# A fused convolution and two-layer MLP on one core: the third chunk's convolution taps added up on VectorE and transposed in blocks

## The chip, the cores and the metric

One core of a Trainium2 chip runs the whole kernel: TensorE (matmuls), VectorE, ScalarE and GpSimd, with SyncE issuing most transfers. The metric is device time in microseconds of one execution; the profile's span is a little shorter than that time. Smaller is better.

## What is computed

```python
def _attn_ref(x, weight_gen):            # x (2, 4096, 192), weight_gen (2, 4096, 8, 7)
    w = exp(weight_gen - max(weight_gen)); w = w / (sum(w) + 1e-09)
    x_unf = x_pad[:, idx, :].reshape(B, S, K, H, group)
    out = np.einsum('bshk,bskhg->bshg', w, x_unf)
def _moe_ref(x, w_gate, w_val, w_out):   # 192 -> 1536 -> 192
    gate = 1.0 / (1.0 + np.exp(-(x @ w_gate)))
    return gate * (x @ w_val) @ w_out
def _moe2_ref(x, w_in, w_out):           # 192 -> 2048 -> 192
    h = x @ w_in
    return h * np.cos(h) @ w_out
```

A convolution with 7 taps whose weights are a softmax per token and head is followed by a gated layer (layer 1) and a layer with h cos h (layer 2), all on 8192 tokens of 192 numbers.

## The kernel before

**Chunks and steps.** The tokens lie 64 to a partition and are worked off in 16 chunks of 512 (`NCH`, `TC` = 4 tokens per partition). A chunk needs its convolved input transposed, features on partitions: the tile `xT`. Layer 1 of a chunk is 12 steps, layer 2 is 8; `segments` (lines 646 to 651) orders them as layer 1 of chunks 0 and 1, then layer 2 of chunk 0, layer 1 of chunk 2, layer 2 of chunk 1, and so on: layer 1 runs two chunks ahead (`LEAD = 2`). All orders are as the code issues them (`manual_schedule`); every engine works its own list in order.

**A step.** Each step is a hidden group of 18 matmuls into two PSUM banks (`hidden`, line 442), then work on the four other engines, then, some steps later, one out group of 10 matmuls in layer 1 and two in layer 2 (`out_matmuls`, line 461). Operands are split in a high part (`gh`, made by ScalarE, line 619) and a low part (`gl`, made by GpSimd, line 620, 128x512 from two SBUF operands) and both are multiplied. Of the ten matmuls the first four read gh, the next two gl. There are four banks for hidden groups (`ps_h`), so a group can start when the group two steps before has been read for the last time; in layer 2 this is VectorE's product at line 609.

**In a layer-2 step** (lines 849 to 870) VectorE rounds (592, 595, 600), ScalarE takes the sine (605), VectorE multiplies twice (609); the first tile's gh and gl follow at once, the second tile's one step later (`pending`). `finish1` ends a chunk's layer 1: two sums on VectorE (471) in the step in which its last out group runs, then a copy on ScalarE (482) with a sum on GpSimd (483), then two splits (123) and three transfers, `exchange` (368), one stage per step (`later`).

**The input of layer 1.** Chunks 0, 1 and 2 keep the seven products of the convolution apart (`conv_products`, line 311: four in a tile `big`, two in `pr`, one in `acc`), and TensorE adds them up by transposing all seven into the same banks: 7 x 16 matmuls by the identity (`transposes`, line 334). ScalarE and VectorE empty these banks (357, 363), and two transfers complete `xT`. For chunk 2 this stands at the last step of chunk 1's layer 1. Chunks 3 to 14 (`by_blocks`, line 490) go another way: VectorE adds the products as they come (308), transposes 32x32 blocks (395), ScalarE and GpSimd split the result in `hb` and `lb` (402, 404), and SyncE places it with 16 transfers of 48 KB and four more between the halves of `xT` (410, 417, 418). `blocks_ops` does that in five stages, one per layer-2 step.

**Shared buffers.** `big` of chunk 2 lies where `xT` of chunk 1's layer 2 comes to lie (tag `xA`, one buffer); `tr` and `hb` take the places of the two `pr`, `lb` that of `acc`.

Of the kernel before, what the change touches and what calls it, by code (L numbers as in the profile page):

```python
# [14 lines left out]
ALU = mybir.AluOpType  # L15
# [14 lines left out]
def dyn_conv_glu_cos_mlp(  # L30
# [11 lines left out]
    nc = tc.nc  # L42
    B, S, D = x.shape
    H, K = weight_gen.shape[2], weight_gen.shape[3]
# [5 lines left out]
    NCH = T // TC  # L50
# [225 lines left out]
    att = {}  # L276
# [12 lines left out]
    def product_tile():  # L289
        return apool.tile([P, TC, D], F32, name="pr", tag="pr", bufs=2)  # L290
# [20 lines left out]
    def conv_products(c):  # L311
# [3 lines left out]
        for k, pr in enumerate(att[c]):  # L315
            tap(c, k, pr)
            yield

    def banks(name):

        return [ps_h.tile([P, N], F32, name=name, tag="h") for _ in range(2)]
# [68 lines left out]

    def blocks_ops(c):

        src = att[c][0]
        tr = product_tile()
        nc.vector.transpose(
            out=tr.rearrange("p t d -> p (t d)").rearrange("p (b t r) -> p b t r", t=TC, r=BL),
            in_=src.rearrange("p t (b r) -> p b t r", r=BL),
        )
        yield
        hi = apool.tile([P, TC, D], F32R, name="hb", tag="pr", bufs=2)  # L400
        lo = apool.tile([P, TC, D], F32R, name="lb", tag="acc", bufs=1)
        nc.scalar.activation(out=hi, in_=tr, func=AF.Copy)
        yield
        nc.gpsimd.tensor_tensor(out=lo, in0=tr, in1=hi.bitcast(F32), op=ALU.subtract)
        xt = xT[1, c] = tpool.tile([P, 2, NQ, N], F32R, name="xT", tag="xB")
        for x, piece in (0, hi), (1, lo):
            v = piece.bitcast(F32).rearrange("p t d -> p (t d)").rearrange("p (q e n) -> p q e n", q=NQ, e=2)
            for e in range(2):
                for b in range(P // BL):
                    nc.sync.dma_start(  # L410
                        out=xt[e * BL:(e + 1) * BL, x, :, b * P:(b + 1) * P].bitcast(F32),
                        in_=v[b * BL:(b + 1) * BL, :, e],
                    )
            yield
        low, top = HALVES
        for x in range(2):
            nc.sync.dma_start(out=xt[top, x, 0:2].bitcast(F32), in_=xt[low, x, 1:3].bitcast(F32))
            nc.sync.dma_start(out=xt[top, x, 2].bitcast(F32), in_=xt[low, x, 0].bitcast(F32))
# [70 lines left out]

    def by_blocks(c):  # L490

        return LEAD < c < NCH - 1

    def finish2(c):
        va, vc = sums(1.0)
# [150 lines left out]
    LEAD = 2  # L646
# [20 lines left out]
    def do_side(k, budget):  # L667
        i = 0
        while i < len(side):
            lo, hi, cst, fn = side[i]  # L670
            if lo > k:
                i += 1
            elif hi > k and cst > budget:
                break
            else:
                side.pop(i)
                fn()
                budget -= cst
# [19 lines left out]
    def run(ops):  # L698
        for f in ops:
            f()  # L700
        ops.clear()

    with tc.manual_schedule():
# [86 lines left out]
        inputs = {seg_start[1, c - 1] + J1 - (1 if c > 1 else AHEAD): c for c in range(1, NCH)}  # L790
# [9 lines left out]
        blocks = None  # L800
# [6 lines left out]
        for k, st in enumerate(steps):  # L807
            layer, c, j = st.layer, st.c, st.j
            ended = None
            if layer == 1:  # L810
                run(pending)
                do_side(k, 2.5 if k < J1 else 2.0 if k < seg_start[2, 1] else 0.5)
                st.mm_hidden()
                old = bool(waiting) and (waiting[0].layer, waiting[0].c) != (layer, c)
                if old or len(waiting) >= 2 and OUTS[j]:
                    ended = out_products()
                st.gate()
                run(late)
                if j == FINAL and final:
                    next(final)  # L820
                if j == st.nj - 1:
                    nc.scalar.activation(out=warm, in_=sin_bias, func=AF.Sin)
                pending.append(st.product1)
                pending.append(lambda st=st: st.halves(0))
                if ended:
                    ended.finish()
                if k in inputs and by_blocks(inputs[k]):
                    blocks = blocks_ops(inputs[k])
                    next(blocks)
                    next(blocks)  # L830
                    pending.pop(0)()
                    out_products()
                    pending.pop(0)()
                    out_products()
                elif k in inputs:
                    c1 = inputs[k]
                    ops = transpose_ops(att[c1], c1)
                    pending.pop(0)()
                    next(ops)
                    if c1 == 1:  # L840
                        next(decoding)
                        run(late)
                    next(ops)
                    out_products()
                    pending.pop(0)()
                    for _ in ops:
                        pass
                    out_products()
            else:
                st.mm_hidden()  # L850
                if blocks and next(blocks, blocks) is blocks:
                    blocks = None
                n = sum(q.layer == 1 for q in waiting)
                for _ in range(-(-n // (2 - j)) if n else len(waiting) >= 2):
                    ended = out_products() or ended
                if final:
                    for at in (0, 0, 3) if c < NCH - 1 else (2, 3, 4, 5):
                        if j == at and next(final, final) is final:
                            final = None
                st.reduce(ended and ended.finish)  # L860
                run(pending)
                st.cosine()
                for i, r in st.tiles_of():
                    st.product2(i, r)
                    if i == 0 or st is steps[-1]:
                        st.halves(i, r)
                    else:
                        pending.append(lambda st=st: st.halves(1))
                do_side(k, 0.5)
                run(late)  # L870
            if todo:
                todo.pop(0).load(nc.sync)
            waiting.append(st)
            if later and not ended and (k < J1 or k >= s2 or j in (3, 5, 7, 9)):
                if next(later[0], later) is later:
                    later.pop(0)
            if layer == 1 and j == st.nj - 2 and c + 2 < NCH:
                load_x(c + 2)
                if c + 4 in group_at and group_at[c + 4] > 2:
                    load_group(group_at[c + 4], "wf")  # L880
            if layer == 2 and c == 0 and j == 5:
                load_group(2, "wf")
# [35 lines left out]
```

## Time and profile before

| | |
|---|---|
| median of 3 runs | 1217.94 us (1216.75 to 1218.92) |
| profiled execution | 1217.96 us, span 1216.2 us |
| granted TensorE clock | 0.992 of full speed |
| TensorE, VectorE busy | 98%, 75% |
| ScalarE, GpSimd busy | 66%, 64% |
| mean DMA rate | 59 GB/s |

The table on the page gives shares over the whole span. Which engine sets the end in a given stretch is read from the timeline and from the waits: an engine that never waits there sets it. In the rows, PE is TensorE's matmuls, PEld its weight loads, DVE VectorE, ACT ScalarE, POOL GpSimd and SPq SyncE's queue.

### The profile page before, as it was taken

How to read it: one execution, taken by the hardware profiler on the slowest of the kernel's cores; microseconds unless marked ns; L12 is line 12 of the kernel's file. 1: busy time of each engine (PE TensorE's matmuls, PEld its weight loads, DVE VectorE, ACT ScalarE, POOL GpSimd, SP SyncE). 2: the span in 40 equal slices, each digit the busy share in tenths (PEclk: the TensorE clock that was granted, in tenths of full speed). 3: DMA queues.
4: the chain of work that ended last, by engine and by line, in shares of the span. 5: the costliest groups of instructions: out<-in, count | busy, mean ns of one | idle time of the engine just before them, and what ended most of it. 6: DMA issues, size and time to landing. Idle time of an engine off the chain costs nothing.

```text
span 1216.2 us, 26799 instructions
## 1 busy us (share of the span) xinstructions
PE 1191.1 (98%) x10624; PEld 1000.3 (82%) x10624; DVE 911.2 (75%) x1274; ACT 797.6 (66%) x1317; POOL 775.3 (64%) x573
## 2 busy tenths in 40 slices
PE   6899999999999999999999999999999999999997
PEld 5688988888888888888888888888888888899885
DVE  7957888777887777887777887776877777682676
ACT  6776847658475665857557585765847667485675
POOL 3968757657576565756656676565757657574563
PEclk8999999999999999999999999999999999999999
DMA  9912104123030311303123140311313132020011
GB/s 252 247 51 77 39 1 106 32 58 68 34 79 15 99 37 47 79 33 64 30 77 60 35 86 13 85 35 56 74 34 65 28 81 44 7 53 1 14 29 26
DMA packets 97246, 71.41 MB, mean 59 GB/s; under 512 B 57444, under 2 KB 80994, under 8 KB 97120
## 3 DMA queue, kind: packets, MB, share of 16 engines
q1 hardware_dynamic: 96208, 68.57, 24.0%
q8 instruction: 83, 1.36, 0.5%
q10 hardware_dynamic: 912, 1.13, 0.4%
q14 instruction: 43, 0.35, 0.1%
HBM read 30.33 MB, written 6.29 MB: 30 GB/s over the span
## 4 chain that ended last, share of the span: by engine, by line
PE 84%; DVE 1%; ACT 1%; issue 0%; POOL 0%; DVEq 0%; ACTq 0%
PE ph L442 47%; PE po L461 37%; DVE wk L581 0%; DVE acc L308 0%; ACT gh L619 0%; DVE pr L282 0%; POOL gl L620 0%; ACT wk L605 0%; DVE wk L592 0%; DVE wk L609 0%; DVE wk L595 0%; PE pf L532 0%; DVE wk L600 0%; DVE gl L620 0%; ACT wk L578 0%
## 5 line engine op out<-in xcount | busy, mean ns | idle before, releaser
L620 POOL TENSOR_TENSOR gl<-wk,gh 128x512 fp32r<-128x512 f32 x446 | 617.8, 1392 | 402.5 <-ACT gh L619 345.6
L442 PE MATMUL ph<-xT,unit 64*128 64x512 f32 x5760 | 764.0, 388 | 5.1 <-DVE wk L581 3.6
L442 PEld LDWEIGHTS ph<-xT,unit 64*128 64x128 f32 x5760 | 599.6, 185 | 112.0 <-DVE wk L581 7.0
L461 PE MATMUL po<-gh,outu 64*128 64x512 f32 x2688 | 547.8, 387 | 2.0 <-ACT gh L619 1.9
L461 PE MATMUL po<-gl,outu 64*128 64x512 f32 x1792 | 467.9, 388 | 3.1 <-POOL gl L620 3.0
L461 PEld LDWEIGHTS po<-gh,outu 64*128 64x128 f32 x2688 | 405.9, 184 | 49.9 <-ACT gh L619 2.7
L619 ACT ACTIVATE gh<-wk 128x512 fp32r<-128x512 f32 (+1 forms) x450 | 283.1, 629 | 222.6 <-DVE wk L581 188.2
L461 PEld LDWEIGHTS po<-gl,outu 64*128 64x128 f32 x1792 | 319.9, 184 | 37.4 <-POOL gl L620 6.2
L581 DVE TENSOR_TENSOR wk<-ph,wk 128x512 f32<-128x512 f32 x192 | 131.8, 687 | 135.3 <-ACT wk L578 128.5
L609 DVE SCALAR_TENSOR_TENSOR wk<-ph,wk 128x512 f32<-128x512 f32 (+1 forms) x258 | 168.5, 687 | 33.7 <-ACT wk L605 33.7
L605 ACT ACTIVATE wk<-wk,sin_bias 128x512 f32<-128x512 f32 (+1 forms) x258 | 172.9, 713 | 28.0 <-DVE wk L595 20.4
L578 ACT ACTIVATE wk<-ph 128x512 f32<-128x512 f32 x192 | 113.5, 591 | 60.6 <-PE ph L442 59.7
L592 DVE TENSOR_SCALAR wk<-ph 128x512 f32<-128x512 f32 x129 | 88.0, 682 | 70.7 <-PE ph L442 70.7
L599 ACT ACTIVATE wk<-ph 128x512 int32<-128x512 f32 x129 | 75.9, 588 | 63.4 <-PE ph L442 62.6
L282 DVE TENSOR_TENSOR pr<-xp,sm 128x768 f32<-128x768 f32 x84 | 105.9, 1262 | 0.0
L308 DVE TENSOR_TENSOR acc<-acc,pr 128x768 f32<-128x768 f32 x78 | 103.7, 1330 | 0.4
L595 DVE SCALAR_TENSOR_TENSOR wk<-wk,ph 128x512 f32<-128x512 f32 x129 | 88.1, 683 | 4.4
L600 DVE TENSOR_TENSOR wk<-wk,ph 128x512 f32<-128x512 int32 x129 | 87.3, 677 | 0.3 <-ACT wk L599 0.3
L471 DVE SCALAR_TENSOR_TENSOR va<-po,va 128x512 f32<-128x512 f32 x32 | 22.0, 688 | 37.5 <-PE po L461 34.3
L505 POOL TENSOR_TENSOR vc<-vc,vs 64x256 f32<-64x256 f32 x30 | 31.3, 1044 | 1.9 <-ACT vs L504 0.8
L470 ACT ACTIVATE va<-po 128x512 f32<-128x512 f32 x32 | 19.1, 597 | 19.3 <-PE po L461 19.0
L123 POOL TENSOR_TENSOR unit<-wf,unit 128x768 fp32r<-128x768 f32 (+1 forms) x11 | 22.2, 2023 | 13.6 <-ACT unit L121 13.6
(68 smaller groups left out, 499.6 us busy)
## 6 DMA issues: line engine op xcount, KB each, us to landing
xT<-xT SPq DMA_DIRECT2D x78, 256.0 KB, 3.8
xp<-in_x_dram SPq DMA_DIRECT2D x13, 960.0 KB, 4.8
out_dram<-o SPq DMA_DIRECT2D x360, 16.0 KB, 1.5
rawo<-in_moe_w_out_dram SPq DMA_DIRECT2D x7, 768.0 KB, 15.9
xT<-hb SPq DMA_DIRECT2D x96, 48.0 KB, 2.0
xT<-lb SPq DMA_DIRECT2D x96, 48.0 KB, 1.9
raw<-in_moe_w_in_dram SPq DMA_DIRECT2D x8, 384.0 KB, 15.9
xT<-xT SPq DMA_DIRECT2D x24, 128.0 KB, 3.6
```

Source lines behind the costliest of these rows:

```text
L282: nc.vector.tensor_tensor(out=out.rearrange("p t (h g) -> p t h g", g=G), in0=xp[c][:, k:k + TC, :].rearrange("p t (h g) -> p t h g", g=G) ...
L308: nc.vector.tensor_tensor(out=acc, in0=acc, in1=last, op=ALU.add)
L442: nc.tensor.matmul(ps[i], lhsT=u.t[r, w, (s + i) % NQ, c0:c0 + P], rhs=xt[r, x, s, :], start=n == 0, stop=n == len(terms) - 1,)
L461: nc.tensor.matmul(po[2 * i + a], lhsT=w[r, d0:d0 + P], rhs=g[r], start=first and g is gh and d0 < D, stop=last and g is gl,)
L578: nc.scalar.activation(out=self.w[0], in_=self.ps[0], func=AF.Sigmoid)
L581: nc.vector.tensor_tensor(out=self.w[0], in0=self.ps[1], in1=self.w[0], op=ALU.mult)
L592: nc.vector.tensor_scalar(out=w, in0=u, scalar1=0.25, scalar2=ROUND_MAGIC, op0=ALU.add, op1=ALU.add)
L595: nc.vector.scalar_tensor_tensor(out=w, in0=w, scalar=ROUND_MAGIC, in1=u, op0=ALU.subtract, op1=ALU.subtract)
L605: nc.scalar.activation(out=w, in_=w, func=AF.Sin, scale=-SIN_SCALE, bias=sin_bias)
L609: nc.vector.scalar_tensor_tensor(out=w, in0=self.ps[i][:, r], scalar=TWO_PI, in1=w, op0=ALU.mult, op1=ALU.mult)
L619: nc.scalar.activation(out=gh, in_=w, func=AF.Copy)
L620: eng.tensor_tensor(out=gl, in0=w, in1=gh.bitcast(F32), op=ALU.subtract)
```

## The change

Chunk 2 goes the way of the later chunks. Its seven products are made as before, in the same places. At the first layer-2 step of chunk 0 VectorE adds the four in `big` to `acc`, at the end of the second step the two `pr`; at the end of the third it transposes, and ScalarE makes `hb`. `lb` and the transfers follow in the fourth to sixth step. The 112 transposing matmuls of chunk 2, four copies on ScalarE, four subtractions on VectorE and two transfers go. Chunk 2's result is written in another order of tokens, with as many transfers of the same size.

```diff
+    def conv_sums(c):
+        for pr in att[c][:-1]:
+            nc.vector.tensor_tensor(out=att[c][-1], in0=att[c][-1], in1=pr, op=ALU.add)
+            yield
...
     def blocks_ops(c):
-        src = att[c][0]
+        src = att[c][-1]
...
     def by_blocks(c):
-        return LEAD < c < NCH - 1
+        return LEAD <= c < NCH - 1
...
                 if k in inputs and by_blocks(inputs[k]):
                     blocks = blocks_ops(inputs[k])
-                    next(blocks)
-                    next(blocks)
+                    if inputs[k] > LEAD:
+                        next(blocks)
+                        next(blocks)
                     pending.pop(0)()
                     out_products()
...
                 st.mm_hidden()
-                if blocks and next(blocks, blocks) is blocks:
+                if blocks and (c > 0 or j > 2) and next(blocks, blocks) is blocks:
                     blocks = None
...
+                if c == 0 and j == 0:
+                    adding = conv_sums(LEAD)
+                    for _ in range(K - 3):
+                        next(adding)
                 st.reduce(ended and ended.finish)
...
+                if c == 0 and j in (1, 2):
+                    for _ in range(2):
+                        next(adding if j == 1 else blocks)
                 do_side(k, 0.5)
```

Lines below the new function stand 5 lower in the changed kernel (620 is 625, 609 is 614).

VectorE, around the first layer-2 steps of chunk 0, before (`pt` are the banks of the transposes, `ph` those of the hidden groups):

```order
L581 TENSOR_TENSOR wk<-ph,wk 128x512 x2
L363 TENSOR_TENSOR xT<-pt,xT 128x4x64 x4
L592 TENSOR_SCALAR wk<-ph 128x512
L595 SCALAR_TENSOR_TENSOR wk<-wk,ph 128x512
L600 TENSOR_TENSOR wk<-wk,ph 128x512
L609 SCALAR_TENSOR_TENSOR wk<-ph,wk 128x512 x2
```

and in the changed kernel, over three steps:

```order
L586 TENSOR_TENSOR wk<-ph,wk 128x512 x2
L321 TENSOR_TENSOR acc<-acc,prs 128x768 x4
L597 TENSOR_SCALAR wk<-ph 128x512
L600 SCALAR_TENSOR_TENSOR wk<-wk,ph 128x512
L605 TENSOR_TENSOR wk<-wk,ph 128x512
L614 SCALAR_TENSOR_TENSOR wk<-ph,wk 128x512 x2
L597 TENSOR_SCALAR wk<-ph 128x512
L600 SCALAR_TENSOR_TENSOR wk<-wk,ph 128x512
L476 SCALAR_TENSOR_TENSOR va<-po_1109,va 128x512
L476 SCALAR_TENSOR_TENSOR vc<-po_1110,vc 128x512
L605 TENSOR_TENSOR wk<-wk,ph 128x512
L614 SCALAR_TENSOR_TENSOR wk<-ph,wk 128x512 x2
```

Four adds stand where the four subtractions stood; two more and the transpose follow behind the second and third step.

GpSimd, the third and fourth layer-2 step of chunk 0, before (two gl per step; `vc` is chunk 1's result of layer 1, `xT_1727` its layer-2 input):

```order
L620 TENSOR_TENSOR gl_1799<-wk_1786,gh_1797 128x512
L483 TENSOR_TENSOR vc_1722<-vc_1722,vs_1804 64x512
L620 TENSOR_TENSOR gl_1800<-wk_1787,gh_1798 128x512
L620 TENSOR_TENSOR gl_1860<-wk_1847,gh_1858 128x512
L123 TENSOR_TENSOR xT_1727<-va_1721,xT_1727 128x512
```

and in the changed kernel:

```order
L625 TENSOR_TENSOR gl_1680<-wk_1667,gh_1678 128x512
L488 TENSOR_TENSOR vc_1601<-vc_1601,vs_1690 64x512
L409 TENSOR_TENSOR lb_1688<-pr_1685,hb_1687 128x768
L625 TENSOR_TENSOR gl_1681<-wk_1668,gh_1679 128x512
L625 TENSOR_TENSOR gl_1756<-wk_1743,gh_1754 128x512
L123 TENSOR_TENSOR xT_1606<-va_1600,xT_1606 128x512
```

The new low piece of chunk 2's input, `lb`, stands ahead of the third step's second gl. ScalarE makes `hb` and then the copy `vs` in the same stretch:

```order
L610 ACTIVATE wk_1668<-wk_1668,sin_bias_92 128x512
L624 ACTIVATE gh_1678<-wk_1667 128x512
L407 ACTIVATE hb_1687<-pr_1685 128x768
L487 ACTIVATE vs_1690<-vc_1601 64x512
L604 ACTIVATE wk_1744<-ph_1694 128x512
L624 ACTIVATE gh_1679<-wk_1668 128x512
```

Before, `hb` was not there and the copy (line 482) came right behind the first gh.

## Rows read from the trace of the kernel before

**Rows 1.** Page, part 1: busy us (share of the span) xinstructions of each engine.
```profile
PE 1191.1 (98%) x10624; PEld 1000.3 (82%) x10624; DVE 911.2 (75%) x1274; ACT 797.6 (66%) x1317; POOL 775.3 (64%) x573
```
**Rows 2.** TensorE's waits, 170 to 1000 us: total us, times, longest.
```profile
PE ph L442 <- DVE wk L581: 0.4, 1, 0.4
```
**Rows 3.** Timeline, TensorE's weight loads: start us, us, engine, line, operation, tiles, xcount.
```profile
109.78 2.34 PEld L334 LDWEIGHTS pt<-ident,prs 64*128 64x128 f32 x62
...
113.47 0.19 PEld L461 LDWEIGHTS po<-gh,outu 64*128 64x128 f32 x1
...
115.68 2.15 PEld L442 LDWEIGHTS ph<-xT,unit 64*128 64x128 f32 x18
...
117.72 0.56 PEld L461 LDWEIGHTS po<-gh,outu 64*128 64x128 f32 x4
...
118.18 0.34 PEld L461 LDWEIGHTS po<-gl,outu 64*128 64x128 f32 x2
...
118.86 2.15 PEld L442 LDWEIGHTS ph<-xT,unit 64*128 64x128 f32 x18
...
134.27 0.33 PEld L461 LDWEIGHTS po<-gl,outu 64*128 64x128 f32 x2
...
147.87 2.15 PEld L442 LDWEIGHTS ph<-xT,unit 64*128 64x128 f32 x18
```
**Rows 4.** Timeline, VectorE, 110 to 127 us; in brackets idle time before, releaser.
```profile
110.99 0.69 DVE L581 TENSOR_TENSOR wk<-ph,wk 128x512 f32<-128x512 f32 x1 [1.43 <-ACT wk L578]
...
118.22 0.69 DVE L592 TENSOR_SCALAR wk<-ph 128x512 f32<-128x512 f32 x1 [1.97 <-PE ph L442]
...
120.42 1.30 DVE L609 SCALAR_TENSOR_TENSOR wk<-ph,wk 128x512 f32<-128x512 f32 x2 [0.19 <-ACT wk L605]
...
121.65 0.68 DVE L592 TENSOR_SCALAR wk<-ph 128x512 f32<-128x512 f32 x1
...
125.64 0.69 DVE L609 SCALAR_TENSOR_TENSOR wk<-ph,wk 128x512 f32<-128x512 f32 x1 [0.19 <-ACT wk L605]
```
**Rows 5.** Timeline, GpSimd, 110 to 133 us.
```profile
110.08 2.49 POOL L620 TENSOR_TENSOR gl<-wk,gh 128x512 fp32r<-128x512 f32 x2
...
112.53 1.97 POOL L183 TENSOR_TENSOR outu<-wf,outu 128x256 fp32r<-128x256 f32 x2
...
114.47 2.52 POOL L620 TENSOR_TENSOR gl<-wk,gh 128x512 fp32r<-128x512 f32 x2
...
131.19 1.28 POOL L483 TENSOR_TENSOR vc<-vc,vs 64x512 f32<-64x512 f32 x1
```
**Rows 6.** Line 308, adds of the later chunks: duration ns min/median/max, first and last start.
```profile
L308 DVE TENSOR_TENSOR acc<-acc,pr x78: 945/1002/2048, 167.9 to 1051.5; 128x768 f32<-128x768 f32 x78
```
**Rows 7.** Line 620, the low pieces gl: the same.
```profile
L620 POOL TENSOR_TENSOR gl<-wk,gh x446: 1259/1295/2092, 28.0 to 1201.9; 128x512 fp32r<-128x512 f32 x149
```
**Rows 8.** Timeline of VectorE, 60 to 124 us.
```profile
86.71 2.03 DVE L282 TENSOR_TENSOR prs<-xp,sm 128x768 f32<-128x768 f32 x1
```
**Rows 9.** Timeline of GpSimd, 60 to 124 us.
```profile
87.89 2.01 POOL L483 TENSOR_TENSOR vc<-vc,vs 64x512 f32<-64x512 f32 x1
...
89.86 1.99 POOL L620 TENSOR_TENSOR gl<-wk,gh 128x512 fp32r<-128x512 f32 x1
```
**Rows 10.** Timeline, 183 to 217 us: the fourth chunk's input.
```profile
186.05 0.97 DVE L395 STREAM_TRANSPOSE pr<-acc 128x768 f32<-128x768 f32 x1
...
189.20 0.83 ACT L402 ACTIVATE hb<-pr 128x768 fp32r<-128x768 f32 x1
...
191.88 1.85 POOL L404 TENSOR_TENSOR lb<-pr,hb 128x768 fp32r<-128x768 f32 x1
```
**Rows 11.** Timeline, ScalarE, copy for chunk 1's sum.
```profile
129.88 0.63 ACT L482 ACTIVATE vs<-vc 64x512 f32<-64x512 f32 x1
```
**Rows 12.** Timeline, SyncE: exchange of chunk 1's layer-2 input.
```profile
140.12 2.96 SPq L368 DMA_DIRECT2D xT<-xT  x3
```
**Rows 13.** Page, part 6: issues, KB each, median us to landing.
```profile
xT<-xT SPq DMA_DIRECT2D x24, 128.0 KB, 3.6
```

## The prediction

> **What bounds the kernel now.** I read the page's busy table first: TensorE is busy 98% of the span, VectorE 75%, ScalarE 66%, GpSimd 64% [rows 1]. A busy share alone does not prove a bound, so the waits of TensorE come next: between 170 and 1000 us it waits for anything only once, 0.4 us [rows 2]. The timeline of TensorE's weight loads then shows what that means here: the groups follow each other without a gap [rows 3]. A hidden group (18 matmuls) takes 117.72 - 115.68 = 2.04 us, an out group (10 matmuls) 118.86 - 117.72 = 1.14 us, and inside an out group the first load that needs the low piece gl comes 118.18 - 117.72 = 0.46 us after its start [rows 3]. So from about 110 us on every microsecond taken off TensorE's queue is one off the end, and every microsecond for which it is made to wait is one added; nothing later has slack to give it back.
>
> I call the last layer-1 steps of the second chunk steps 8 to 11, and the eight layer-2 steps of the first chunk steps 0 to 7. Times are those of the profiled execution, 1217.96 us over a span of 1216.2; the median of the runs shown is 1217.94, so the sum can be set against either. A measurement of this kernel can tell about 0.2% (2.4 us) from no change.
>
> **What is taken away.** The 112 transposing matmuls stand between 109.78, when the first weights are loaded, and 113.47, when the next out group begins [rows 3]: 3.69 us of TensorE with no gap, all of it on the path. The four copies on ScalarE and the four subtractions on VectorE that emptied their banks go too, as do two exchange transfers; VectorE sits idle on either side of that work (it ends 110.99 + 0.69 = 111.68 and starts step 0 at 118.22 [rows 4]), so I price them at nothing.
>
> **First price: the cover of the transposes.** Without them the out group of step 8 begins at 109.78 and wants its gl at 110.24. GpSimd makes the gl of steps 8 and 9 from 110.08 on, two in 2.49 us [rows 5], so the first is done at 111.33: a wait of 1.09. The group ends at 109.78 + 1.14 + 1.09 = 112.01; step 9's gl is wanted at 112.47 and done at 112.57, 0.10 more. Step 0's hidden group starts at 113.25 instead of 115.68. Of 3.69 us, **2.43 are left**.
>
> **Second price: four adds against GpSimd.** They follow VectorE's last layer-1 product at 111.68. Alone an add takes 0.95 us, but the same instruction in the later chunks goes up to 2.05 [rows 6], and GpSimd's gl goes from 1.26 to 2.09 [rows 7]. Rows of both engines show why: a product that starts at 86.71 on VectorE ends at 88.74, while GpSimd's next instruction, begun at 87.89, lasts 2.01 and the one after begins at 89.86 [rows 8, 9]. They take turns: GpSimd's starts lie 1.97 us apart instead of 1.26, so each VectorE instruction with two operands in SBUF pushes GpSimd back by 0.71 us, and it ends 0.85 us after GpSimd is done with the instruction ahead of it (88.74 against 87.89, where GpSimd took up its next). The Trainium skill (SBUF — State Buffer, "Who interferes with whom") says so outright: a VectorE instruction with two SBUF inputs and a GpSimd instruction that reads SBUF exclude each other, and the later one blocks until the first is done. By that rule the adds cost what these rows say; taken as free of each other, the sum below would end 5 us lower (second rival).
>
> From 112.57 GpSimd has four instructions queued and no gap until 114.47 + 2.52 = 116.99: two low pieces of an output weight, then the gl of steps 10 and 11 [rows 5]. One add goes ahead of each. The gl of step 10 ends at 114.47 + 2.52/2 + 3 x 0.71 = 117.86, that of step 11 at 116.99 + 4 x 0.71 = 119.83, and the fourth add 0.85 behind the former: **VectorE is free at 118.7**, not at 115.5. TensorE's hidden group 0 ends at 115.29; the out group of step 10 wants its gl at 115.75 and waits 2.11. Hidden group 1 then starts at 118.54 (before: 118.86): 0.3 of the gain is left.
>
> **Third price: VectorE is late from step 0 on.** The banks of hidden group 2 are those of step 0, free when its last product is done. Step 0 took VectorE 118.22 to 121.72, 3.50 us, and the next began 3.43 after it; step 1, with the two sums of the finished chunk in it, took 121.65 to 126.33, 4.68 [rows 4]. Now step 0 runs from 118.7 to 122.2, so hidden group 2 starts at 122.2 (before: 118.86 + 2.04 + 1.14 = 122.04): the gain is gone. Step 1 ends at 118.7 + 3.43 + 4.68 = 126.8. The two adds behind it meet the gl of steps 0 and 1, and I take both at the contended end, 2.0 each (bounds 0.95 and 2.05 [rows 6]): 130.8. Step 2, of the form of step 0, ends at 134.3.
>
> **Fourth price: a chain through three engines to step 2's second gl.** On GpSimd that gl now stands behind the sum for chunk 1 (line 483 before) and the new low piece lb; the copy on ScalarE that feeds this sum stands behind hb; and hb waits for the transpose. So after step 2: transpose 0.97, hb 0.83 [rows 10], ScalarE's copy 0.63 [rows 11], the sum 1.28 [rows 5], lb 1.85 [rows 10], gl 1.25 [rows 5], together 6.81: done at 134.3 + 6.8 = 141.1. TensorE loaded weights for that gl at 134.27 [rows 3]. With hidden group 4 held to 134.3 by the banks, TensorE comes there at 134.3 + 2.04 + 1.14 + 0.46 = 137.9 and waits the rest. From there it runs dense again: **141.1 - 134.27 = 6.8 us later than before**.
>
> **What I price at nothing, and its cover.** The new input's 20 transfers stand on SyncE's queue around the three that exchange chunk 1's input. Those take 2.96 us to issue [rows 12] and wait for GpSimd's low piece of vc, five GpSimd instructions (some 6.3 us) behind the late gl: 147.4 to 150.4. The last four follow at some 0.6 us each and land 3.6 us later [rows 13]: the two that the first matmuls read by about 154.6, the others by 155.8. The first matmul of chunk 2 was at 147.87 [rows 3], now at 154.7, and reads the others 12 matmuls (1.4 us) later. This just fits; up to 2 us if it doesn't. The new output order of chunk 2 keeps the number and size of its transfers.
>
> **The sum,** as TensorE's place against before: -3.69 us for the transposes, -2.43 at hidden group 0 after the two waits, -0.32 at group 1 after the wait for step 10's gl, +0.2 at group 2, held by the banks, and +6.8 at step 2's second gl and from there to the end: 1217.96 + 6.8 = **1224.8 us**. Bounds: with adds at 0.95 throughout it is +1.9 (second rival). If GpSimd's queued instructions always go first, the four adds all come after 116.99 and end at 120.8 instead of 118.7: +8.9, 1226.9.
>
> **The rivals.**
> *Faster.* The adds fill VectorE's idle stretch and the new input is hidden, as the four copies were: only the cover is lost, 1217.96 - 2.43 = 1215.5. For it speaks the idle time from 111.68 to 118.22. Against it: the gl of step 2 would have to be done by 134.27 - 2.43 = 131.8, so VectorE done with step 2 by 125.0, while three steps and six free adds behind 111.68 already pass that. Decisive is the order on GpSimd: if the gl were not behind lb. Chance 5%.
> *No change that can be told.* The adds meet no GpSimd instruction. Step 0 is then bound by its hidden group (113.25 + 2.54 = 115.8); 115.8 + 3.43 + 4.68 + 1.9 + 3.5 = 129.3, and with 6.8 of chain 136.1: +1.9, 1219.8. For it: many of the later adds do run in 0.95. Against it: GpSimd has no gap from 110.08 to 116.99 for them to meet. 14% with partial cases.
> *Slower by the placement as well.* The exchange and the last four transfers miss the start of chunk 2: up to 2 us more, 1226.8. For it speaks that its margin above is a tenth of a microsecond; against it, that of the later chunks' inputs, placed in the same way, none makes TensorE wait [rows 2]. 15%, within the slower cases.
>
> **How the numbers follow.** My forecast and its neighbours (one to all of the contended adds, with and without late placement) have 81%: 1220.4 to 1227.6. The range takes in the free adds, 1219.3 to 1227.6. Chances: faster by over 0.2% 0.05, within 0.2% 0.14, slower by over 0.2% 0.81; the likeliest case's own range is 1222 to 1227.
>
> **What would show it.** In the changed profile: no transposes near 110; TensorE waiting for gl for about 1 us at 110 and again about 2 us near 116; adds of 1.4 to 2 us and GpSimd's low pieces of 2 us between 112 and 120; step 0 on VectorE starting near 118.7; and, decisive, a wait of 2 to 4 us of TensorE for a gl near 138 to 141, with sum and lb ahead of it on GpSimd. Chunk 2's first hidden group should start near 154.7. If TensorE doesn't wait at the second tile of step 2, the fourth price is wrong; if the adds take 0.95, the second is.

## The result and the profile after

The changed kernel takes **1224.68 us** (median of 4 runs, 1224.58 to 1225.75) against 1217.35 us for the kernel before in the same comparison: ratio 1.0061, 95% interval [1.0047, 1.0075]. It is slower by 0.6%. The profiled execution took 1224.58 us, its span is 1222.8 us.

The busy table of the page answers to [rows 1]: 112 matmuls fewer, about the same busy time, and a span 6.6 us longer.

```profile
PE 1190.4 (97%) x10512; PEld 985.2 (81%) x10512; DVE 921.1 (75%) x1277; ACT 797.7 (65%) x1314; POOL 780.8 (64%) x574
```

TensorE's two longest kinds of wait from 100 to 170 us (total us, times, longest); before, it waited for nothing between 110 and 150 us:

```profile
PE po L466 <- POOL gl L625: 4.2, 3, 2.5
PE ph L447 <- DVE wk L614: 1.4, 1, 1.4
```

The timeline of its weight loads puts them in place (a load's wait comes out a little longer than its matmul's, 2.93 against 2.5 us for the longest); it answers to [rows 3]. One thing must be known to compare the two: this execution runs 1.03 us ahead of the one before when it comes here (VectorE's last layer-1 product starts at 109.96 instead of 110.99 [rows 4]). The lead arises near 60 us, where both kernels run the same instructions; the last section comes back to it.

```profile
110.37 0.19 PEld L466 LDWEIGHTS po<-gl,outu 64*128 64x128 f32 x2 [0.98 <-POOL gl L625]
...
112.19 2.01 PEld L447 LDWEIGHTS ph<-xT,unit 64*128 64x128 f32 x18
...
116.22 0.19 PEld L466 LDWEIGHTS po<-gl,outu 64*128 64x128 f32 x2 [1.57 <-POOL gl L625]
...
116.79 2.01 PEld L447 LDWEIGHTS ph<-xT,unit 64*128 64x128 f32 x18
...
121.80 0.18 PEld L447 LDWEIGHTS ph<-xT,unit 64*128 64x128 f32 x1 [1.86 <-DVE wk L614]
122.42 3.12 PEld L447 LDWEIGHTS ph<-xT,unit 64*128 64x128 f32 x17 [0.43 <-DVE wk L614]
...
133.25 1.68 PEld L447 LDWEIGHTS ph<-xT,unit 64*128 64x128 f32 x16 [0.43 <-DVE wk L614]
...
140.04 0.29 PEld L466 LDWEIGHTS po<-gl,outu 64*128 64x128 f32 x2 [2.93 <-POOL gl L625]
...
141.06 3.09 PEld L447 LDWEIGHTS ph<-xT,unit 64*128 64x128 f32 x18
146.46 2.00 PEld L447 LDWEIGHTS ph<-xT,unit 64*128 64x128 f32 x18
...
155.07 2.00 PEld L447 LDWEIGHTS ph<-xT,unit 64*128 64x128 f32 x18
```

Read it as a ledger against before, with the 1.03 us taken into account. Hidden group 0 starts at 112.19, 2.46 us better than 115.68. Group 1, at 116.79, is 1.04 better. Group 2 waits for VectorE and the gain is gone; group 4 waits for it again, at 133.25. At 140.04 TensorE gets the second gl of step 2 that it got at 134.27: 5.77 + 1.03 = 6.80 us later. The groups behind it follow without a wait that was not there before, the first of them slowly (last section); chunk 2's first group starts at 155.07 with no wait for a transfer.

VectorE's timeline (it answers to [rows 4]) shows who was late:

```profile
109.96 0.69 DVE L586 TENSOR_TENSOR wk<-ph,wk 128x512 f32<-128x512 f32 x1 [1.44 <-ACT wk L583]
110.57 8.37 DVE L321 TENSOR_TENSOR acc<-acc,prs 128x768 f32<-128x768 f32 x4
118.87 0.68 DVE L597 TENSOR_SCALAR wk<-ph 128x512 f32<-128x512 f32 x1
...
126.87 2.91 DVE L321 TENSOR_TENSOR acc<-acc,pr 128x768 f32<-128x768 f32 x2
...
131.90 1.30 DVE L614 SCALAR_TENSOR_TENSOR wk<-ph,wk 128x512 f32<-128x512 f32 x2 [0.20 <-ACT wk L610]
133.12 0.97 DVE L400 STREAM_TRANSPOSE pr<-acc 128x768 f32<-128x768 f32 x1
```

And GpSimd's, which answers to [rows 5]:

```profile
111.53 2.70 POOL L183 TENSOR_TENSOR outu<-wf,outu 128x256 fp32r<-128x256 f32 x2
114.19 3.94 POOL L625 TENSOR_TENSOR gl<-wk,gh 128x512 fp32r<-128x512 f32 x2
...
135.69 1.28 POOL L488 TENSOR_TENSOR vc<-vc,vs 64x512 f32<-64x512 f32 x1 [1.00 <-ACT vs L487]
136.94 1.81 POOL L409 TENSOR_TENSOR lb<-pr,hb 128x768 fp32r<-128x768 f32 x1
138.72 2.52 POOL L625 TENSOR_TENSOR gl<-wk,gh 128x512 fp32r<-128x512 f32 x2
```

Four adds take 8.37 us where four free ones would take 3.8, and GpSimd's pairs go from 1.97 to 2.70 and from 2.52 to 3.94 us. Behind step 2, GpSimd stands idle for 1.00 us until ScalarE's copy `vs` comes, then does the sum and lb, and only then the gl that TensorE waits for.

### The profile page after: what moved, and what is told of

It is laid out like the page before. It is cut to its first block, busy times and chain, and to the rows that moved or that the text cites. A ratio compares the mean times of both kernels' runs of the same rounds, so it can differ in the third digit from the quotient of the medians.

```text
span 1222.8 us, 26606 instructions
## 1 busy us (share of the span) xinstructions
PE 1190.4 (97%) x10512; PEld 985.2 (81%) x10512; DVE 921.1 (75%) x1277; ACT 797.7 (65%) x1314; POOL 780.8 (64%) x574
## 4 chain that ended last, share of the span: by engine, by line
PE 83%; DVE 1%; ACT 1%; issue 0%; POOL 0%; DVEq 0%; ACTq 0%
PE ph L447 47%; PE po L466 37%; DVE wk L586 0%; DVE acc L308 0%; ACT gh L624 0%; DVE pr L282 0%; POOL gl L625 0%; ACT wk L610 0%; DVE wk L597 0%; DVE wk L614 0%; DVE wk L600 0%; DVE wk L605 0%; DVE gl L625 0%; ACT wk L583 0%; PE pf L537 0%
## 5 line engine op out<-in xcount | busy, mean ns | idle before, releaser
L466 PEld LDWEIGHTS po<-gh,outu 64*128 64x128 f32 x2688 | 400.7, 184 | 53.1 <-ACT gh L624 3.3
L466 PEld LDWEIGHTS po<-gl,outu 64*128 64x128 f32 x1792 | 315.1, 184 | 45.3 <-POOL gl L625 11.9
```

The costliest lines, as they stand in the source:

```text
L466: nc.tensor.matmul(po[2 * i + a], lhsT=w[r, d0:d0 + P], rhs=g[r], start=first and g is gh and d0 < D, stop=last and g is gl,)
```

## The experiments

Letters of theories are defined anew in each expectation. The first four runs take the change apart; the others test the reading by using it.

**The change without its six adds.** The line in `conv_sums` goes, so six of the seven taps are left out of chunk 2's input; everything else stays.

```diff
     def conv_sums(c):
         for pr in att[c][:-1]:
-            nc.vector.tensor_tensor(out=att[c][-1], in0=att[c][-1], in1=pr, op=ALU.add)
             yield
```

> The changed kernel without its six adds (chunk 2's input is one tap's product alone; the other six taps are left out), all else as in the change. Theory A, the prediction's: the adds, by their turns with GpSimd and the late VectorE behind them, are what pushes the chain; without them step 2 on VectorE ends at 115.8 + 3.43 + 4.68 + 3.5 = 127.4, the chain of 6.8 us to the second gl ends at 134.2 against 134.27 before: 1217 to 1218.5 us, with one wait of TensorE of 2 to 2.5 us left at that gl, and about 1 us at 110. Rival C, that the order on GpSimd and ScalarE (hb, lb and the sum ahead of that gl) alone makes the loss: 1222 us or more.

Measured: 1218.66 us (1217.62 to 1219.52), ratio 1.0006 [0.9997, 1.0016]. With the adds, 6 of the 7 us are gone. What is left of the change, 112 matmuls fewer and 3.69 us less for TensorE to do, gains nothing: TensorE waits 0.98 and 0.26 us near 111 us, as priced, and then here, in its weight loads:

```profile
133.32 0.18 PEld L465 LDWEIGHTS po<-gl,outu 64*128 64x128 f32 x2 [2.34 <-POOL gl L624]
133.89 3.48 PEld L446 LDWEIGHTS ph<-xT,unit 64*128 64x128 f32 x18
```

The chain behind step 2 costs 2.34 us even where VectorE is not late, and the group behind it is slow (last section).

**Reductions in place of the adds.** Six instructions as long as an add, but with one operand: each sums groups of four neighbours of one product, which is not the sum of the taps.

```diff
-            nc.vector.tensor_tensor(out=att[c][-1], in0=att[c][-1], in1=pr, op=ALU.add)
+            four = pr.rearrange("p t (d w) -> p (t d) w", w=4)
+            nc.vector.tensor_reduce(out=att[c][-1][:, 0], in_=four, axis=AX.X, op=ALU.add)
```

> The six adds replaced by six reductions of the same 768 numbers per partition, one operand in SBUF instead of two (chunk 2's input is then not the sum of the taps). Theory A: these don't take turns with GpSimd, so each takes about 0.9 us, GpSimd's low pieces near 112 to 117 keep 1.25 us, VectorE starts step 0 when its hidden group is there, step 2 ends near 129.2 and the chain at 136.0: +1.8 us, about 1219 us. Rival B, that it is VectorE's time as such and not the turns with GpSimd: as the changed kernel, 1224 to 1225 us.

Measured: 1221.68 us (1219.52 to 1223.45), ratio 1.0033 [1.0020, 1.0047], 3 us under the change. VectorE, GpSimd and TensorE's weight loads:

```profile
111.86 3.91 DVE L322 TENSOR_REDUCE acc<-prs 128x192 f32<-128x768 f32 x4
114.76 2.54 POOL L626 TENSOR_TENSOR gl<-wk,gh 128x512 fp32r<-128x512 f32 x2
129.45 1.93 PEld L448 LDWEIGHTS ph<-xT,unit 64*128 64x128 f32 x17 [0.43 <-DVE wk L615]
...
136.26 0.29 PEld L467 LDWEIGHTS po<-gl,outu 64*128 64x128 f32 x2 [2.95 <-POOL gl L626]
...
137.28 3.05 PEld L448 LDWEIGHTS ph<-xT,unit 64*128 64x128 f32 x18
```

Four of them take 3.91 us (0.98 each) instead of 8.37, and the pair of gl beside them 2.54 instead of 3.94. So it is the second operand that makes the two engines meet; these reductions also write only a quarter of what an add writes, but the one of the best version below writes as much and is as free of GpSimd. The Trainium skill (SBUF — State Buffer, "Who interferes with whom") says that on this chip a VectorE reduction never contends with GpSimd. These rows agree. The wait behind step 2 stays, and the time is 2.7 us over the first theory's 1219: that theory had left out TensorE's lowered clock behind the wait (the group at 137.28, last section), 1.4 us of it. Two free reductions behind step 1 are not hidden either: TensorE waits 0.43 us for VectorE at 129.45.

**hb and lb behind step 2's second gl.** GpSimd's queue is put in the order that the fourth price blames it for not having.

```diff
-                if blocks and (c > 0 or j > 2) and next(blocks, blocks) is blocks:
+                if blocks and (c > 0 or j > 3) and next(blocks, blocks) is blocks:
...
                 run(pending)
+                if c == 0 and j == 3:
+                    for _ in range(2):
+                        next(blocks)
                 st.cosine()
...
-                    for _ in range(2):
+                    for _ in range(2 if j == 1 else 1):
                         next(adding if j == 1 else blocks)
```

> The changed kernel with hb and lb one step later in the order, behind step 2's second gl; adds and transpose where they were. Theory A: the wait at that gl shrinks by the 2.7 us of hb and lb, but lb then stands ahead of step 3's gl and the transfers start some 3 us later, so about 2 us come back: 1222 to 1223.5 us. Rival C: the order was the whole cause: 1218 us or less. If the transfers are late, TensorE waits at chunk 2's first hidden group, up to 2 us, and the time is that of the change.

Measured: 1225.07 us (1224.18 to 1226.38), ratio 1.0066 [1.0049, 1.0082], the time of the change. The wait for that gl falls from 2.93 to 0.49 us, hidden group 5 starts at 137.85 instead of 141.06, and what is gained is lost again, most of it at chunk 2's first hidden group, in TensorE's waits from 100 to 170 us:

```profile
PE po L466 <- POOL gl L625: 2.6, 3, 1.1
PE ph L447 <- DMA xT<-xT: 1.8, 1, 1.8
```

SyncE's last transfer of this `xT`, in the change and in this run:

```profile
152.05 0.60 SPq L423 DMA_DIRECT2D xT<-xT  x1
```
```profile
152.81 0.60 SPq L423 DMA_DIRECT2D xT<-xT  x1
```

Part of the loss is this run's own: with hb and lb later, the transfers are issued 0.76 us later too. The rest is the placement. TensorE comes to that group at 152.04 instead of 155.07, and the transfers that were in time for the change are not in time for this. So the placement is a second chain not much shorter than the first, and mending one of them alone brought nothing here.

**The adds alone.** The kernel before with the six adds in the places of the change, their sum unused.

```diff
+    def conv_sums(c):
...
+                if c == 0 and j == 0:
+                    adding = conv_sums(LEAD)
+                    for _ in range(K - 3):
+                        next(adding)
                 st.reduce(ended and ended.finish)
...
+                if c == 0 and j == 1:
+                    for _ in range(2):
+                        next(adding)
                 do_side(k, 0.5)
```

> The kernel before, transposes on TensorE kept, with the six adds put in at the change's two places (their sum is not used). Theory A: the first four run behind the emptying of the transposes' banks, from 116.3 to about 120.8; step 0 on VectorE ends at 124.3, hidden group 2 is 2.3 us late; step 1 and two adds of 1.5 to 2 us, step 2 ends at 135 to 136, hidden group 4 waits until then: 4.5 to 6.5 us later than before, 1222 to 1224 us. Rival C: the adds are hidden in VectorE's idle time: 1217 to 1218 us.

Measured: 1222.48 us (1221.46 to 1222.71), ratio 1.0039 [1.0024, 1.0054]. Here the adds stand behind the four subtractions and meet GpSimd only in part (four take 4.68 us, where free ones would take 3.8, and two 2.92, where 1.9), yet they cost 4.6 us; VectorE's adds and two of TensorE's waits:

```profile
116.32 4.68 DVE L321 TENSOR_TENSOR acc<-acc,prs 128x768 f32<-128x768 f32 x4
...
128.92 2.92 DVE L321 TENSOR_TENSOR acc<-acc,pr 128x768 f32<-128x768 f32 x2
```
```profile
123.85 0.18 PEld L447 LDWEIGHTS ph<-xT,unit 64*128 64x128 f32 x1 [1.52 <-DVE wk L614]
...
134.70 0.18 PEld L447 LDWEIGHTS ph<-xT,unit 64*128 64x128 f32 x1 [1.12 <-DVE wk L614]
```

In step 1 VectorE needs 4.68 us [rows 4] and TensorE about 4.3 from one group to the next, in step 2 3.4 to 3.5 against 4.3: little room is left, and what is put between these steps shows up as waits of TensorE, here and, with less, in the run with the free reductions.

**A version that goes round all three.** The reading so far says: sum with one operand, do nothing of it between layer-2 steps, and have lb done before step 0's gl. So chunk 2's taps are written into three places of `big`, two reductions over three terms run in chunk 1's layer 1, a third right behind VectorE's last layer-1 product, with transpose, hb and lb behind it. The whole sum is formed. The edit against the change:

```diff
+        if c == LEAD:
+            att[c] = [big, acc_tile()]
+            for k, slot in enumerate((0, 1, 2, 1, 2, 1, 2)):
+                tap(c, k, big[:, slot])
+                yield
+                if k == 2:
+                    total(big[:, 0:3], big[:, 3])
+                    yield
+                if k == 4:
+                    total(big[:, 1:4], big[:, 0])
+                    yield
+            return
...
+    def total(terms, out):
+        nc.vector.tensor_reduce(
+            out=out.rearrange("p t d -> p (t d)"), in_=terms.rearrange("p k t d -> p (t d) k"), axis=AX.X, op=ALU.add
+        )
...
                     pending.pop(0)()
+                    if inputs[k] == LEAD:
+                        total(att[LEAD][0][:, 0:3], att[LEAD][1])
+                        next(blocks)
+                        next(blocks)
                     out_products()
...
+                at = [14, 14, 15, 16, 17, 18, 19, 20, 21] if c == LEAD else TAPS0
```

The last line says by which step each of the nine pieces is due. The adds of the change go, and `blocks_ops` runs its last three stages in steps 0 to 2, as for the later chunks.

> The whole sum is formed, but by one-operand reductions: the first three taps and the next two in layer 1 of the second chunk (taps due earlier), the last three terms in VectorE's idle stretch after its last layer-1 product, with the transpose, hb and lb right behind, before step 0. Nothing of it then stands between VectorE and step 1 or ahead of step 2's second gl. Theory A (the loss of the change is the adds against GpSimd plus the chain behind step 2, both of place, not of kind): final reduction about 2.5 us from 111.7, transpose about 115, lb in GpSimd's idle time after 117; no wait of TensorE above 0.5 us after step 0; what is left is the cover, so 1217.9 - 2.4 = 1215.5, and up to 2 us more where the earlier taps and reductions delay layer 1 of the second chunk (1215.5 to 1217.9). Theory B (any waits of TensorE near 110 to 117 draw a lowered clock, which costs about 1 us, as in the runs without adds): 1216.5 to 1218, no gain that can be told. Theory C (the block way costs this chunk something of its own, such as placement late): TensorE waits for xT at the third chunk's first hidden group and the time is above 1218.5.

Measured: 1217.37 us (1216.81 to 1218.59), ratio 0.9998 [0.9989, 1.0007]. From 110 to 1200 us TensorE's waits are those of before, and hidden group 0 is 3.6 us better placed against the groups ahead of it than before. But those groups had come 3.2 us late: in layer 1 of chunk 1 a tap on VectorE took 4.37 us and TensorE waited for the product behind it,

```profile
95.49 1.91 PEld L459 LDWEIGHTS ph<-xT,unit 64*128 64x128 f32 x17 [3.00 <-DVE wk L598]
```

**Half of it.** The kernel before, with the first five taps summed by the same two reductions, so that TensorE transposes three tiles instead of seven; taps and reductions as in the run above, with the same due steps.

```diff
+        if c == LEAD:
+            att[c] = [big[:, k] for k in range(3)]
...
         att[c] = [big[:, k] for k in range(K - 3)] + [product_tile(), product_tile(), acc_tile()]
```

> The kernel before, with the first five taps summed by two reductions in layer 1 of the second chunk, so that TensorE transposes three tiles instead of seven: 64 matmuls fewer. The 112 took 3.69 us, so 64 are 2.1 us. Transposes of 1.6 us still cover the 1.09 us for which GpSimd's gl would be late. Theory A (TensorE's queue is the bound behind 110 us and the cover matters only below 1.1 us): -2.1 us against before, 1215.8, less what two reductions of some 2.5 us each and the earlier taps delay in layer 1 of the second chunk (0 to 2 us). Theory B (cover matters for more, VectorE being what sets step 0): less than 1 us gained, 1217 to 1218.

Measured: 1219.78 us (1218.62 to 1221.11), ratio 1.0014 [1.0006, 1.0023]: a miss. It has the same loss ahead of 110 us (hidden group 11 is 4.15 us late) and regains 2.0 us there, which is the price of 64 matmuls.

**The control: taps due earlier and nothing else.**

```diff
-                at = [k1 + i * (last - k1) // n for i in range(n)] if c == LEAD else TAPS0
+                at = [14, 14, 15, 17, 18, 20, 21] if c == LEAD else TAPS0
```

> The control for the two others: the kernel before with the seven taps due earlier and nothing else. It shows what the earlier taps are worth by themselves in layer 1 of the second chunk, where TensorE waits 5.9 us in 9 waits for gl and for VectorE's products. Same time as before within 1 us is expected (1217 to 1219): the taps meet GpSimd instructions in either place. If it is faster by over 1 us, gains of the other two belong to the taps' place and not to the sums.

Measured: 1220.34 us (1216.73 to 1221.24), ratio 1.0019 [1.0010, 1.0028], about 2.4 us slower, which I had not expected. The largest piece is one tap on VectorE, with GpSimd in the same time:

```profile
89.06 5.52 DVE L282 TENSOR_TENSOR prs<-xp,sm 128x768 f32<-128x768 f32 x1
```
```profile
88.05 1.30 POOL L620 TENSOR_TENSOR gl<-wk,gh 128x512 fp32r<-128x512 f32 x1
89.31 1.99 POOL L183 TENSOR_TENSOR outu<-wf,outu 128x256 fp32r<-128x256 f32 x2
91.27 1.28 POOL L620 TENSOR_TENSOR gl<-wk,gh 128x512 fp32r<-128x512 f32 x1
92.52 1.25 POOL L123 TENSOR_TENSOR xT<-va,xT 128x512 fp32r<-128x512 f32 x1
```

GpSimd works off five instructions at the pace of one that meets nobody, and VectorE's tap ends 0.8 us behind the last of them: it was passed over four times.

**Three other placings of the same nine pieces.** Only the due steps differ: one a step; the taps due as in the kernel before; and the first pieces in VectorE's idle stretches of steps 13 and 14.

```diff
-                at = [14, 14, 15, 16, 17, 18, 19, 20, 21] if c == LEAD else TAPS0
+                at = [14, 15, 16, 17, 18, 19, 20, 21, 22] if c == LEAD else TAPS0
...
+                at = [15, 16, 17, 18, 18, 19, 20, 20, 21] if c == LEAD else TAPS0
...
+                at = [13, 14, 14, 15, 16, 17, 18, 19, 21] if c == LEAD else TAPS0
```

> As the early sums, but the nine pieces (seven taps, two reductions) fall due one a step, steps 14 to 22 of layer 1. In the early sums TensorE kept all that the transposes had cost (3.6 us at the hidden group behind them) and waited for nothing after it, but had lost 4.2 us between 87 and 110 us, where taps met GpSimd (one took 4.37 us). Theory A (that loss is of the taps' place, and can be avoided): the loss before 110 us falls to 0 to 2 us, the gain behind it stays at 3.6: 1214.3 to 1216.3. Theory B (VectorE and GpSimd are full in that stretch, and two reductions of 2.8 us have to be paid for there wherever they stand): 1217 to 1218.5 as before.

> As the early sums, but the taps fall due as in the kernel before (steps 15 to 21), with the reductions behind the third and fifth. Theory A: the early taps alone cost 2.4 us (control run), so without them the time is 1217.4 - 2.4 = 1215. Theory B (full stretch): 1217 to 1218.5.

> As the early sums, with the first four pieces in steps 13 and 14, where VectorE has idle stretches of 4 and 2 us, and the rest one a step. Theory A: less to do in the crowded stretch from 86 us on: 1214.5 to 1216.5. Theory B: 1217 to 1218.5.

Measured: 1217.98 us (ratio 0.9999 [0.9990, 1.0008]), 1221.14 us (1.0034 [1.0021, 1.0046]) and **1213.76 us** (0.9968 [0.9955, 0.9980]). The first two miss what their first theory said; the last is better than its own, and beats both kernels, by 0.3% and 0.9%. In the first, the last tap starts at 110.25 on VectorE, so step 0 starts late there and TensorE waits 1.28 and 0.67 us at hidden group 2. In the second, two reductions stand among the late taps and one product of VectorE keeps TensorE waiting 4.0 us at 108.4. In the last, TensorE comes to 110 us no later than before; VectorE, GpSimd and TensorE's weight loads from there:

```profile
110.39 2.84 DVE L332 TENSOR_REDUCE acc<-prs 128x768 f32<-128x2304 f32 x1
113.27 0.98 DVE L412 STREAM_TRANSPOSE pr<-acc 128x768 f32<-128x768 f32 x1
114.60 0.69 DVE L609 TENSOR_SCALAR wk<-ph 128x512 f32<-128x512 f32 x1 [0.35 <-POOL gl L637]
```
```profile
111.36 1.98 POOL L183 TENSOR_TENSOR outu<-wf,outu 128x256 fp32r<-128x256 f32 x2
...
115.82 1.84 POOL L421 TENSOR_TENSOR lb<-pr,hb 128x768 fp32r<-128x768 f32 x1
```
```profile
112.04 2.18 PEld L459 LDWEIGHTS ph<-xT,unit 64*128 64x128 f32 x18
```

The pair for the output weight beside the reduction takes 1.98 us, as with nothing beside it before (1.97 [rows 5]). Reduction and transpose end at 114.25, before step 0's hidden group is done; lb runs where GpSimd has nothing else; hidden group 0 starts at 112.04 instead of 115.68, and these 3.64 us last to the end (the last hidden group starts 3.61 earlier).

**The chain alone.** The version just told, with transpose, hb and lb put back to the places of the change.

```diff
                         total(att[LEAD][0][:, 0:3], att[LEAD][1])
-                        next(blocks)
-                        next(blocks)
...
-                if blocks and next(blocks, blocks) is blocks:
+                if blocks and (c > 0 or j > 2) and next(blocks, blocks) is blocks:
...
+                if c == 0 and j == 2:
+                    next(blocks)
+                    next(blocks)
```

> The first-taps kernel (1213.8 us) with transpose, hb and lb put back to the places of the change (end of the third layer-2 step, fourth step), and nothing else: the chain through three engines without the adds and without a late VectorE. There VectorE ends step 2 at 126.1 and TensorE wants the second gl of step 2 at 130.7 us, without a wait. Theory A (the fourth price, the queue order behind step 2): gl done 6.8 us behind VectorE, at 132.9, so TensorE waits 2.2 us there and the time is 1216.0, up to 1217.1 if a lowered clock follows the wait. Theory B (the chain costs only because VectorE comes late): no wait there above 0.5 us, 1213.8 to 1214.3.

Measured: 1216.36 us (1215.16 to 1217.31), 2.6 us over the version it is made from. VectorE, GpSimd, TensorE's weight loads:

```profile
124.91 1.30 DVE L626 SCALAR_TENSOR_TENSOR wk<-ph,wk 128x512 f32<-128x512 f32 x2 [0.20 <-ACT wk L622]
```
```profile
131.77 2.52 POOL L637 TENSOR_TENSOR gl<-wk,gh 128x512 fp32r<-128x512 f32 x2
```
```profile
133.08 0.19 PEld L478 LDWEIGHTS po<-gl,outu 64*128 64x128 f32 x2 [2.23 <-POOL gl L637]
```

The gl is done at 131.77 + 2.52/2 = 133.03, 6.82 us behind the end of step 2 (126.21), and TensorE waits 2.23: the fourth price by itself, with nothing late ahead of it.

**Its control.** The kernel before with the seven taps due as early, and all 112 transposes.

```diff
-                at = [k1 + i * (last - k1) // n for i in range(n)] if c == LEAD else TAPS0
+                at = [13, 14, 14, 16, 17, 19, 21] if c == LEAD else TAPS0
```

> The kernel before with its seven taps due as early as in the first-taps kernel and nothing else: no sums, 112 transposes as before. Theory A (the gain of the first-taps kernel is the 3.7 us of transposes): same as before or up to 2.5 us slower, as the other control, 1217 to 1220.5. Theory B (the gain is of the taps' place): 1214 to 1215.5.

Measured: 1218.45 us (1216.73 to 1219.62), ratio 1.0006 [0.9998, 1.0015]. The early taps alone gain nothing, so the gain of 4 us needs the transposes gone; 3.6 us of it are the 3.69 that they took.

## Why the prediction was right

It said 1224.8 us for the profiled execution or the median, slower with a chance of 0.81; it is 1224.58 and 1224.68. By its own steps, with the 1.03 us of lead taken off its times:

- **First price, the cover: right.** Waits of 0.98 and 0.25 us for 1.09 and 0.10, and 2.46 us left at hidden group 0 for 2.43.
- **Second price, adds against GpSimd: right in kind, wrong in order.** It let the engines take turns, one add ahead of each of GpSimd's four instructions, with VectorE free at 118.7 (117.7 here) and a wait of 2.11 us for step 10's gl. VectorE was free at 118.94, 1.3 us later: the pair for the output weight grew by 0.73 us, one turn instead of two, so one add went behind GpSimd's queue instead of into it (one by one the adds take 2.51, 1.93, 1.90 and 1.93 us: the first let the first of that pair pass). The first gl came sooner (wait 1.57) and VectorE later.
- **Third price, VectorE late from step 0 on: right in its end.** Hidden group 2 waits for VectorE as said, longer than said (1.86 and 0.43 us, where its numbers give 0.5). The two adds behind step 1 were taken at 2.0 each and took 2.91 together, and that gives the 1.1 us back: step 2 ends at 133.20, forecast 134.3 - 1.0 = 133.3. Two errors of a microsecond cancelled, which is luck.
- **Fourth price, the chain: right.** 133.20 to 139.98 is 6.78 us for 6.81, and TensorE is 6.80 us later at that gl for 6.8. The chain run alone gave 6.82.
- **Priced at nothing, the placement: no wait, but with help.** The last four transfers were to follow at some 0.6 us each; SyncE took from 148.93 to 152.65 us for them, 3.7 instead of 2.4. They were in time all the same, but TensorE came to chunk 2's first hidden group at 155.07, not at 153.7: its lowered clock had cost it 1.4 us on the way. The third of the four, issued at 150.88, lands 4.6 us later, at 155.45. By the prediction's 1.4 us the matmuls that read it would have been due at 155.1 without that loss: an estimate, but by it the margin came from there, and no run shows it alone.
- **Not in the sum:** TensorE's lowered clock behind its wait for that gl, 1.4 us (last section). In the profiled pair the kernel before had lost 1.0 us in the same way near 60 us and lost 0.6 us more behind its last hidden group (which starts 7.2 us later in the change), so that the forecast of +6.8 met a span of +6.6 and a median of +7.3. That the time came out within 0.2 us is luck; the chain and its length are not.

Of the rivals, *Faster* fails with the adds gone and the chain left, where the change only breaks even. The order on GpSimd, said to be decisive, is not enough: with gl ahead of lb the time was that of the change. But its premise can be had: with a sum of one operand, placed early, the block way keeps all 3.6 us and even the loss of cover doesn't come (no wait near 110 us in that version).

## What to carry to other kernels

Before work goes into an engine's idle time, ask who its queue neighbours are in that time and what comes behind it: here the adds cost 6 us between the steps, as many one-operand reductions there 3, and the whole sum, made by reductions ahead of the steps, left a gain of 4 in the best of its places. Count the operands that VectorE reads from SBUF; in this kernel a reduction over several terms did the work of two-operand adds without meeting GpSimd. And price each chain that ends at the bound engine: where two are nearly as long, mending one may show nothing.

## What had not been expected of the hardware

**VectorE does not get its turn for certain.** Where VectorE and GpSimd meet, the kernel before showed turns, each pushing GpSimd back by 0.71 us [rows 8, 9]. In the run with the taps due earlier, a waiting tap was passed over by instructions that GpSimd took up later, and took 5.52 us. The Trainium skill (SBUF — State Buffer, "Who interferes with whom") says that the later one blocks until the first is done. Here the tap came second (89.06 against 88.05) and did block, but on past the end of the first (89.35), through four more of GpSimd's, which is not what that sentence says. The first add of the change, passed over once, is the same in small. What decides between turns and passing over stays open. It is part of why moving the same nine pieces by up to three steps took the time from 1213.8 to 1221.1 us.

**Behind some of its waits TensorE's clock is lower.** Granted clock (column PEclk) of the change in two stretches, each right behind a wait, and of both kernels from 60 to 70 us, the change first (columns: busy us and instructions of PE, PEld, DVE, ACT, POOL, then PEclk, DMA share, GB/s):

```profile
122.00:128.00 6.00, 5.88 (x35) 4.50 (x36) 5.74 (x10) 5.36 (x10) 3.69 (x3) 0.72 0.02 4
...
140.00:146.00 6.00, 5.96 (x38) 4.83 (x40) 3.22 (x6) 3.78 (x7) 6.00 (x5) 0.72 0.35 74
```
```profile
60.00:70.00 10.00, 9.80 (x164) 9.25 (x160) 4.87 (x8) 7.12 (x14) 7.09 (x5) 1.00 0.35 96
```
```profile
60.00:70.00 10.00, 10.00 (x155) 10.00 (x153) 3.63 (x7) 5.83 (x12) 6.97 (x5) 0.83 0.15 31
```

Before the change the first two stretches stand at 1.00. A mean of 0.72 is a part at 1.2 GHz and the rest at 2.4. Behind 140.04 TensorE takes 1.02 us to the next hidden group instead of 0.68 (134.27 to 134.95 before), and that group 146.46 - 141.06 = 5.40 us to the one after instead of 4.31: 1.43 us together. The third and fourth rows are the lead of 1.03 us: there the kernel before was lowered in this execution and the change was not, on the same instructions. What decides it stays open, and a wait's length alone does not: 2.34 us was followed by a slow group (3.48 us of loads) in the run without adds, 2.23 us in the chain run was not. So some 1 us of either sign can be in a comparison of two single executions here, and effects of that size need the medians.
